# Storing the last 64 rows of a batch pair: one Pool transfer over 128 partitions in place of two Sync transfers over 64

## The chip, the cores and the metric

The kernel runs on one core of one Trainium2 chip. The metric is the device time of one execution in microseconds. Executions of the kernel before take 435.15 to 436.84 us on the days and chips here. The profile's span, from the first to the last instruction, is some 1.7 to 2.2 us shorter than the time. Times of the span below are counted from its start.

## The reference

The program is an attention layer with a forget gate (8 batches, 8 heads, 576 rows, head width 64), followed by a spectral mix over the sequence and a small gate:

```python
    u = x + y                                   # x: attention output, y: irfft of the mixed modes
    return (u + np.maximum(u @ w_ch, 0.0)).astype(np.float32)     # (8, 576, 512)
```

Only this last line and its output matter here. The output is 8 x 576 x 512 float32, 9.4 MB. As 576 = 4 x 128 + 64, each batch has four blocks of 128 rows and one of 64.

## The kernel before: the parts that matter

The last stage works through a list of jobs. A wide job makes one 128-row block of two batches. A job `(b, 4)` makes the last 64 rows of batches b and b+1 in one tile: the lower 64 partitions hold batch b, the upper 64 batch b+1.

```python
        jobs = []
        for b in range(0, B, 2):
            if b == 0:
                jobs += [((c, sb), (c, sb + 1)) for c in (b, b + 1) for sb in (0, 2)]
            else:
                jobs += [((b, sb), (b + 1, sb)) for sb in range(4)]
        jobs += [((b, 4),) for b in range(0, B, 2)]        # last: four jobs of 64 + 64 rows
...
        def emit_o(job, ps, u, o, pair, split=False):
            ...
                nc.vector.scalar_tensor_tensor(o[:, bs, :], ps[1][:, bs, :], 0.0, u[:, bs, :], ALU.max, ALU.add)
                b, sb = job[0]
                if sb == 4:
                    for h in range(2):
                        nc.sync.dma_start(
                            out[b + h, 512:576, :], o[64 * h : 64 * h + 64, 0, :]
                        )
                ...
                elif sb % 2 or n_wide < 2:                 # the wide stores, on Sync too
```

`pool_dma` is a helper that issues a transfer on Pool and keeps it in program order. Pool loads the weights (`wb`) with it and, in the stage before the last one, moves ten small rows (`yl` to `yy`).

The softmax here doesn't subtract the row's maximum and nothing guards it: scores larger than these inputs give would overflow.

## Time and profile before

| | kernel before |
|---|---|
| time, median | 435.68 us (435.57 to 436.04, 5 runs) |
| span of the profiled run | 434.1 us |
| last arithmetic ends | 425.7 us |
| last output data | 432.5 us |
| DMA rate 420 to 424 us / 428 to 432 us | 401 / 221 GB/s |

The prediction shows the lines for these.

### The profile page before, as it was taken

Reading aid. Unit: us, or ns where it says so; the run is one execution under the profiler, and the core shown is the slowest. Engines: PE = TensorE matmul, PEld = TensorE weight load, DVE = VectorE, ACT = ScalarE, POOL = GpSimd, SP = SyncE. Lnnn points to the kernel's source line nnn. Section 1 sums busy time; section 2 is a strip of 40 time slices with the busy share of each in tenths; the row PEclk is TensorE's granted clock in tenths of the full one; section 3 lists DMA queues with packets and bytes.
Section 4 is the critical chain, followed back from the end, with each engine's and each line's share of the span. In section 5 each row is a group of like instructions: output and inputs, shape, how many; then the busy total and the mean of one; then the engine's idle time right before and its main releaser. Section 6 shows DMA issues by size and latency. Waiting matters only on the chain.

```text
span 434.1 us, 12383 instructions
## 1 busy us (share of the span) xinstructions
PE 360.6 (83%) x5338; PEld 249.1 (57%) x5356; DVE 263.5 (61%) x659; ACT 225.5 (52%) x339; POOL 126.9 (29%) x198
## 2 busy tenths in 40 slices
PE   3787799999887977878878797899999977989991
PEld 2353666676665665666656576666665544644540
DVE  5797788876565656555557667533324543743891
ACT  2887478774645446446365454244344432731780
POOL 7333332233233232332323232232232232200400
PEclk9997699997967958668688659699999998989996
DMA  8999999999999999999999999999999999996798
GB/s 181 236 235 237 238 237 238 246 213 217 228 220 237 220 229 232 216 237 227 222 236 212 211 211 211 211 211 213 210 211 211 210 211 211 211 211 130 256 384 257
DMA packets 51086, 97.39 MB, mean 224 GB/s; under 512 B 3799, under 2 KB 12983, under 8 KB 51031
## 3 DMA queue, kind: packets, MB, share of 16 engines
q0 software_dynamic: 46464, 85.65, 101.0%
q1 hardware_dynamic: 4567, 10.95, 7.2%
q8 instruction: 42, 0.69, 0.6%
q14 instruction: 13, 0.11, 0.1%
HBM read 163.73 MB, written 9.44 MB: 399 GB/s over the span
## 4 chain that ended last, share of the span: by engine, by line
DMA 36%; PE 30%; ACT 9%; DVE 8%; issue 4%; POOL 0%; ACTq 0%; DVEq 0%
DMA wb<-in_moe_w_i_dram 36%; ACT E L590 7%; PE pav L628 6%; PE A L191 5%; PE tp L321 5%; PE ps L583 4%; PE vp L555 2%; PE pu L842 2%; DVE QTs L336 2%; ACT KT L334 2%; PE px L671 1%; PE pz L842 1%; DVE os L1019 1%; DVE x_all L650 1%; DVE E L605 1%
## 5 line engine op out<-in xcount | busy, mean ns | idle before, releaser
L590 ACT ACTIVATE E<-ps 128x1024 bf16<-128x1024 f32 (+1 forms) x128 | 100.8, 847 | 27.1 <-PE pav L628 17.1
L191 PE MATMUL A<-XT,wb 128*128 128x16 bf16 x1984 | 71.7, 181 | 11.7 <-DMA wb<-in_moe_w_i_dram 7.1
L191 PEld LDWEIGHTS <-wb 128*128 128x128 bf16 x1984 | 64.2, 99 | 26.0 <-issue 12.2
L96 POOL DMA_DIRECT2D wb<-in_moe_w_r_dram x64 | 42.5, 665 | 120.9 <-PE ps L583 22.0
L96 POOL DMA_DIRECT2D wb<-in_moe_w_i_dram x64 | 42.3, 661 | 85.8 <-DMA wb<-in_moe_w_i_dram 40.1
L583 PE MATMUL ps<-QTs,KT 64*128 64x64 bf16 (+4 forms) x384 | 53.7, 312 | 14.6 <-ACT E L590 12.4
L628 PE MATMUL pav<-va,E 128*128 128x65 bf16 (+1 forms) x1088 | 53.7, 205 | 7.2 <-DVE x_all L650 6.8
L628 PEld LDWEIGHTS <-E 128*128 128x128 bf16 (+1 forms) x1088 | 43.8, 111 | 16.9 <-DVE x_all L650 8.4
L605 DVE TENSOR_TENSOR E<-E,trimask 128x256 bf16<-128x256 bf16 (+2 forms) x128 | 37.0, 304 | 20.0 <-ACT E L590 19.4
L881 ACT CAST XW<-pxw 128x512 bf16<-128x512 f32 x36 | 20.7, 587 | 34.8 <-PE pxw L874 23.4
L340 ACT COPY VT<-tp 128x640 bf16<-128x640 bf16 (+1 forms) x32 | 23.3, 759 | 28.8 <-PE tp L321 28.7
L583 PEld LDWEIGHTS <-KT 64*128 64x128 bf16 x384 | 19.2, 98 | 31.5 <-issue 20.6
L924 ACT CAST XW<-pB 128x512 bf16<-128x512 f32 x36 | 20.9, 586 | 29.8 <-PE pB L842 29.7
L334 ACT COPY KT<-tp 128x640 bf16<-128x640 bf16 (+1 forms) x32 | 22.0, 750 | 26.1 <-PE tp L321 26.0
L923 DVE CAST x_all<-pA 128x512 bf16<-128x512 f32 x36 | 24.9, 692 | 15.4 <-PE pA L842 13.6
L874 PE MATMUL pxw<-wch,yy 128*128 128x512 bf16 x133 | 32.9, 379 | 1.1 <-issue 0.5
L336 DVE COPY QTs<-tp 128x640 bf16<-128x640 bf16 (+1 forms) x32 | 23.3, 767 | 14.1 <-PE tp L321 13.9
L650 DVE TENSOR_TENSOR x_all<-pav,rcp 128x384 bf16<-128x384 f32 x64 | 29.1, 455 | 1.1
L639 DVE RECIPROCAL rcp<-pav 128x6 f32<-128x6 f32 x64 | 12.3, 192 | 25.1 <-PE pav L628 24.3
L842 PEld LDWEIGHTS <-ident_bf 64*64 64x64 bf16 (+1 forms) x336 | 15.6, 109 | 18.4 <-issue 10.7
L555 PE MATMUL vp<-ident_bf,VT 128*128 128x128 bf16 x215 | 21.9, 254 | 5.1 <-DVE QTs L336 4.6
L156 DVE TENSOR_TENSOR YTe<-A,Yacc 128x128 bf16<-128x128 f32 x16 | 5.9, 369 | 32.2 <-PE A L191 32.2
(142 smaller groups left out, 619.1 us busy)
## 6 DMA issues: line engine op xcount, KB each, us to landing
wb<-in_moe_w_r_dram POOLq DMA_DIRECT2D x62, 512.0 KB, 16.9
wb<-in_moe_w_i_dram POOLq DMA_DIRECT2D x62, 512.0 KB, 17.4
stv<-in_v_dram POOLq DMA_DIRECT2D x9, 576.0 KB, 15.6
out_dram<-os SPq DMA_DIRECT2D x10, 512.0 KB, 5.0
stk<-in_k_dram POOLq DMA_DIRECT2D x11, 288.0 KB, 15.6
stq<-in_q_dram POOLq DMA_DIRECT2D x11, 288.0 KB, 15.4
wx<-in_v_dram POOLq DMA_DIRECT2D x5, 576.0 KB, 16.2
out_dram<-uo SPq DMA_DIRECT2D x3, 512.0 KB, 3.2
```

What stands on the lines that cost most here:

```text
L96: keep(nc.gpsimd.dma_start(dst, src))
L191: ins = nc.tensor.matmul(A[:, eb, mi, :], lhsT=w_of(mi, eb * 128), rhs=x_of(m), start=(i == 0), stop=(i == len(terms) - 1),)
L334: nc.scalar.copy(rows(KTs[pr % 2][:, :, 0:S]), tv)
L336: ins = nc.vector.tensor_copy(rows(QT[pr][:, :, :]), tv)
L555: nc.tensor.transpose(vp[:, sc, :, :].rearrange("p b d -> p (b d)"), VTs[s // 2 % 2][:, h, sc * 128 : (sc + 1) * 128], ident_bf[:, :],)
L583: nc.tensor.matmul(ps[:, b, o : o + n], lhsT=KTs[pr % 2][bs, h, jb * 128 : (jb + 1) * 128], rhs=QT[pr][bs, h, jb * 128 + c0 : jb * 128 + c ...
L590: nc.scalar.activation(E[:, :, piece * 512 : piece * 512 + w], ps[:, :, 0:w], ACT.Exp, scale=scale,)
L605: nc.vector.tensor_tensor(dg, dg, tr, ALU.mult)
L628: nc.tensor.matmul(pav[64 * half : 64 * half + w, slot, :], lhsT=E[:, b, c : c + (w - 1) * st + 1 : st], rhs=va[:, jb, b, :], start=(n == ...
L650: nc.vector.tensor_tensor(xo, pi, ri, ALU.mult)
L842: return nc.tensor.matmul(p, lhsT=lhsT, rhs=rhs, start=first, stop=not first, skip_group_check=True)
L874: nc.tensor.matmul(pxw[:, :], lhsT=xT[:, eb, i * 128 : (i + 1) * 128], rhs=wch[:, eb, :], start=(eb == 0), stop=(eb == NDC - 1),)
```

## The change

The intent is to use all 128 partitions in one transfer, to halve the number of issues, and to free Sync.

```diff
                 if sb == 4:
-                    for h in range(2):
-                        nc.sync.dma_start(
-                            out[b + h, 512:576, :], o[64 * h : 64 * h + 64, 0, :]
-                        )
+                    pool_dma(out[b : b + 2, 512:576, :], o[:, 0, :])
```

The source is 128 partitions x 512. The destination is 2 batches x 64 rows x 512: the two batches do not lie next to each other, so the destination can't be walked as 128 equal steps.

## The prediction

> **What bounds the kernel now.** The change touches four groups of stores at the very end, so I read only the tail: first the chain of waits, then the timeline, then the windows and the DMA view.
>
> The chain's last piece (start us, length us, what):
>
> ```profile
> 8 pieces in order of time: start us, us, what
> ...
> 424.99 0.69 DVE uo L1019
> ```
>
> All arithmetic is over at 424.99 + 0.69 = 425.68 us, but the span is 434.1 us. The last 8.4 us hold stores alone; the chain does not follow them. The timeline of the same stretch:
>
> ```profile
> 422.79 1.90 SPq L1039 DMA_DIRECT2D out_dram<-os  x2
> 424.79 6.25 SPq L1026 DMA_DIRECT2D out_dram<-uo  x8
> ```
>
> L1026 is the changed line: eight stores of 64 rows of 2 KB (128 KB). The first could be ready at 422.68 + 0.68 = 423.36, but Sync is still at the wide stores of L1039 until 424.69. Next, the windows (columns: PE, PEld, DVE, ACT, POOL busy; PE clock; DMA share; GB/s):
>
> ```profile
> 411.00:413.00 2.00, 1.74 (x32) 0.89 (x31) 2.00 (x3) 1.66 (x3) 0.00 (x0) 1.00 1.05 381
> 420.00:424.00 4.00, 3.92 (x44) 1.54 (x37) 3.83 (x5) 3.62 (x6) 0.00 (x0) 1.00 1.02 401
> 424.00:427.25 3.25, 0.65 (x5) 0.13 (x3) 1.52 (x3) 0.12 (x1) 0.00 (x0) 0.88 1.02 406
> 428.00:432.00 4.00, 0.00 (x0) 0.00 (x0) 0.00 (x0) 0.00 (x0) 0.00 (x0) 0.50 0.93 221
> 432.50:434.10 1.60, 0.00 (x0) 0.00 (x0) 0.00 (x0) 0.00 (x0) 0.00 (x0) 0.50 0.02 5
> ```
>
> From 420 to 427.25 the DMA engines are full at about 400 GB/s: they work off the wide stores, and the first 64-row stores queue behind these. From about 427.4 to 432.4 the engines are still 93% occupied, but move only 221 GB/s. Then 1.7 us pass in landing and closing. The DMA view of two windows shows that packet size is not the reason. First 411 to 413, where stores of 2 KB rows over 128 partitions run, then 428 to 432, 2 KB rows over 64 partitions:
>
> ```profile
> q1 hardware_dynamic: 390, 0.74, 100.2%
> ```
>
> ```profile
> q1 hardware_dynamic: 526, 0.88, 92.7%
> ```
>
> The first gives 2 us x 16 engines x 1.002 / 390 = 82 ns a packet, the second 4 x 16 x 0.927 / 526 = 113 ns. Same packet, 1.4 times the time (both counts include small semaphore packets). So the bound of the tail is **how fast the 1.05 MB of 64-row stores drain**: 1.05 MB / 0.21 MB per us = 5.0 us, against 2.7 us at the 381 GB/s of the first window. One caution: Sync's own issue is close behind.
>
> ```profile
> L1026 SPq DMA_DIRECT2D out_dram<-uo x8: 525/591/1254, 424.8 to 430.4; - x8
> ...
> DMA to landing us min/median/max: 2.3/2.6/4.1
> ```
>
> 128 KB per 0.59 us is 222 GB/s, so an issue limit and a drain limit are nearly the same number here.
>
> **What the Trainium skill says.** (1) "SBUF — State Buffer", section "Door 1: The DMA port swizzle": partitions 0 to 63 and 64 to 127 each reach only 8 of 16 ports, with an asymptote of about 218 GB/s against 436 for all 128. The trace agrees: 221 against 381 to 406. This is the intent of the change. (2) "DMA: Bandwidth & Descriptors", section "Why a DMA increments its semaphore by 16 and not by 1", on how many engines a transfer uses: the largest number up to 16 that divides the slowest dimension of both access patterns; the software path gives "some direct copies" all 16. The new transfer has a destination of 2 batches x 64 rows and a source of 128 partitions: the rule gives **2 engines**, one per batch, and consecutive engines for the next transfer. No run here shows it yet: every Pool transfer of the kernel before has equal outer counts of 16 or more. (3) The same page, "Issuing engines are not separate DMA queues": Pool's and Sync's transfers share the same 16 engines, so Pool saves issue time alone. (4) "Perfetto Trace Analysis", section "DMA Instruction — SWDGE (GPSIMD)": the end of a Pool transfer in the profile is the end of descriptor writing, not of the data. The trace agrees: 487 ns in the row below, but 1.6 to 3.1 us to landing.
>
> ```profile
> L837 POOL DMA_DIRECT2D yy<-yl x10: 487/487/512, 402.1 to 406.4; - x10
> ```
>
> **The change part by part.** Removed: eight Sync issues, 6.25 us on Sync from 424.79 on. Added: four Pool issues of 256 KB. Pool has been idle since 406.9, so each issue starts right after its DVE result: 423.36, 424.2, 424.9 and 425.68. I take 0.5 to 0.67 us each (the 487 ns above; 661 to 665 ns for the 512 KB weight loads) plus some 0.7 us to the first byte; the fourth moves data from about 427.0. The arithmetic, PE, DVE and ACT are untouched, and no later tile waits for these four buffers. Bytes are the same.
>
> The data, with 2 engines for each transfer (my main case). At 424.0 there are 2.48 MB left, 1.05 of it the 64-row stores, so 1.43 MB of wide stores, 89 KB an engine. At 401 / 16 = 25 GB/s an engine that takes 3.6 us, to 427.5. The four transfers sit on eight engines, 64 rows x 2 KB = 131 KB each, and all have arrived by 427.5, so it does not matter in which order an engine serves its two queues: each of the eight carries 89 + 131 KB. At 82 ns a row the 131 KB take 5.3 us; at the 23 GB/s an engine that 0.74 MB over 2 us gives, 5.7 us; if an engine alone is a little quicker, 5 us. The last data comes at 427.5 + 5.3 = **432.8** (432.4 to 433.2), against 432.4 before. The ports no longer bind, but half of the engines stand idle: the gain is given straight back, to +0.4 us.
>
> The close. Before, the last landing seen by Sync is at 433.0, the end at 434.1. Pool adds something: its drain.
>
> ```profile
> L1155 POOLq DRAIN  x3: 46/102/4721, 406.1 to 433.8; - x3
> ```
>
> The 4721 ns one ends at 410.8, 3.9 us after Pool's last issue (406.88) and 1.3 us after that transfer had landed (409.5). If it counts from the issue, it ends at about 430.3 and is hidden. If it counts from the landing, it ends some 1.3 us after 433.3 or so, and the close slips by about 1 us. I give the second 40%. Sum in the main case: 434.1 + 0.4 (data) + 0.4 (weighted drain) = 434.9 of span, +0.8 us, so 436.5 of time.
>
> **The rivals.** *All 16 engines (22%).* If the Pool transfer is spread over all engines, 1.05 MB drain at about 380 GB/s in 2.7 us: last data 427.5 + 2.7 = 430.2, a gain of 2.2 us, or 1.2 if the drain costs its 1 us: 433.5 to 434.5. For it: the page's exception, and that the change was made on Pool. Against: the page's rule, by which the outer count of 2 decides. *The drain waits for the landing:* above; +1 us on whichever case. *The four transfers fall on the same two engines (3 to 4%):* 4 x 5.3 = 21 us after 427.5, less what overlaps with the wide stores, so an end near 447 to 449 and a loss of 3%. Nothing in the profile speaks for it; the page's cursor speaks against. *Issue was the bound, not the ports:* then freeing Sync helps the transfer, and the number of engines decides all the same, so it moves nothing in the sum.
>
> **Range and chances.** The whole disputed stretch is 5 us of 434, 1.2%; even removing the slow drain completely cannot reach 2%. The mix is 436.5 with about three quarters of the weight and 434 with a fifth, so I say 436.0. The range runs from the full 16-engine gain (433.4) to slower packets plus the whole drain (437.5). Faster by over 2%: 1%. Slower by over 2%: 4%, the same-engines case. Within 2%: 95%.
>
> **What would show it.** In the profile after: (a) L1026 gone from Sync, four Pool transfers of 0.5 to 0.7 us between 423.4 and 426.5; (b) the DMA share in 428 to 432 near 0.5 with about 200 GB/s, if eight engines carry it at full pace; near 1.0 with 380 GB/s and over by 430.3, if all sixteen do; (c) issue to landing of the Pool transfers 6 us or more in the main case, about 4 in the other; (d) Pool's long drain: its end against the last landing tells the two readings apart. I am wrong if the data ends before 431 (engine count), after 435 (engines shared or slower packets), or if anything before 423 us moves.

## More of the kernel before

One more view helps to compare with the kernel after: the DMA strip of the stretch from 423 to 442 us in 40 slices of 0.475 us. The first row is the busy share of the 16 DMA engines in tenths, the second the rate.

```profile
DMA  9999999998999999898500000000000000000000
GB/s 379 397 405 414 414 414 414 414 405 263 259 233 233 224 229 211 194 211 203 121 17 0 0 0 0 0 0 0 0 0 0 0 0 0 0 0 0 0 0 0
```

The reader sees two plateaus: about 410 GB/s until 427.3 us (wide stores), then 194 to 263 GB/s until 432 us (64-row stores), both with the engines nearly always busy.

## The result, and the profile after

The time went from 435.68 us to **443.15 us** (442.82 to 443.66, 5 runs). Ratio 1.0172, interval 1.0157 to 1.0187: slower by 7.5 us, outside the range of 433.4 to 437.5. By the 2% rule it still counts as the same. (A ratio here is the mean time of one kernel's runs over that of the other's of the same rounds, so it is not quite the ratio of the medians quoted.)

The order of work is unchanged: the last arithmetic starts at 425.06 us (before: 424.99). The same DMA strip for the kernel after:

```profile
DMA  9999999498996555937393433354454200000000
GB/s 379 380 397 405 371 431 397 122 193 243 311 277 174 115 90 89 115 97 113 104 130 121 129 112 121 164 181 164 173 132 63 44 9 0 0 0 0 0 0 0
```

The windows of the kernel after (columns as in the prediction; the last two are DMA share and GB/s):

```profile
424.00:428.00 4.00, 0.73 (x6) 0.14 (x3) 1.60 (x3) 0.20 (x1) 2.98 (x4) 1.00 0.94 321
428.00:432.00 4.00, 0.00 (x0) 0.00 (x0) 0.00 (x0) 0.00 (x0) 0.00 (x0) 0.69 0.68 141
432.00:436.00 4.00, 0.00 (x0) 0.00 (x0) 0.00 (x0) 0.00 (x0) 0.00 (x0) 0.50 0.47 132
436.00:440.00 4.00, 0.00 (x0) 0.00 (x0) 0.00 (x0) 0.00 (x0) 0.00 (x0) 0.50 0.24 63
```

The second plateau is gone. As Pool's data starts, the slice from 426.3 us shows only 122 GB/s. The rate comes back to 311 while wide stores are left; from 429 us until 437 it is 89 to 181 GB/s, and in the windows from 432 us on less than half of the engines are busy. The last data comes at 438.4 us. Pool's timeline, and the DMA view of 423 to 442 us for the kernel after:

```profile
423.74 3.26 POOL L96 DMA_DIRECT2D out_dram<-uo  x4 [16.77 <-DVE uo L1019]
```

```profile
DMA packets 2655, 3.01 MB, mean 159 GB/s; under 512 B 1923, under 2 KB 1923, under 8 KB 2655
## 3 DMA queue, kind: packets, MB, share of 16 engines
q1 hardware_dynamic: 543, 1.95, 29.4%
q0 software_dynamic: 2112, 1.06, 24.9%
...
out_dram<-uo POOLq DMA_DIRECT2D x4, 256.0 KB, 13.4
```

Pool's four transfers were issued one after the other from the first DVE result on, as predicted (0.80 to 0.85 us each), but took 13.4 us from issue to landing in the median. And its queue shows 2,112 packets for 512 rows of 2 KB. In the trace's packet records they are 256 packets of 4 KB (two rows each), 64 of 4 bytes (16 for each transfer) and **1,792 of 8 bytes**. No other store in the kernel before or after has such 8-byte packets. 1,792 is 4 x 448, and 448 is 14 x 32: it fits 14 idle engines that each get as many fillers as one of the two working engines has 4 KB packets (64 rows, two to a packet). I call them fillers; what they are for, no view shows, and the records don't name the engine. Each is recorded at 8 ns in the median, 15.7 us in all, which is 1.0 us for each of 16 engines: by their recorded time alone they would not cost much.

Last, the end. The kernel after, its closing line, and Sync's wait:

```profile
L1152 SPq EVENT_SEMAPHORE  x11: 17/28/28, 439.0 to 441.2; - x11
L1152 POOLq DRAIN  x3: 46/102/14419, 426.0 to 441.0; - x3
```

Pool's long drain starts at 426.0 and ends 14.4 us later, at 440.4: 2.0 us after the last data, while Sync's first event after the landing is at 439.0. In the kernel before, whose long Pool drain was over at 410.8, the close took 434.1 - 432.5 = 1.6 us after the last data; now it takes 441.2 - 438.4 = 2.8 us. Of the 7.1 us of span, 5.9 are data and 1.2 are the close.

### The profile page after: what moved, and what is told of

Same layout as the page of the kernel before. It is cut to its first block, busy times and chain, and to the rows that moved or that the text cites. A ratio compares the mean times of both kernels' runs of the same rounds, so it can differ in the third digit from the quotient of the medians.

```text
span 441.2 us, 12397 instructions
## 1 busy us (share of the span) xinstructions
PE 364.8 (83%) x5356; PEld 249.9 (57%) x5356; DVE 264.4 (60%) x659; ACT 225.7 (51%) x339; POOL 129.3 (29%) x202
## 4 chain that ended last, share of the span: by engine, by line
PE 33%; DMA 24%; ACT 10%; DVE 9%; issue 8%; POOL 2%; POOLq 0%; ACTq 0%
DMA wb<-in_moe_w_i_dram 22%; ACT E L590 7%; PE pav L628 6%; PE A L191 6%; PE ps L583 5%; PE tp L321 5%; PE vp L555 3%; PE px L671 2%; DMA stv<-in_v_dram 2%; DVE QTs L336 2%; ACT KT L334 2%; DVE XT L685 2%; DVE E L605 1%; DVE x_all L650 1%; POOL yy L837 1%
## 5 line engine op out<-in xcount | busy, mean ns | idle before, releaser
L590 ACT ACTIVATE E<-ps 128x1024 bf16<-128x1024 f32 (+1 forms) x128 | 100.9, 848 | 28.3 <-PE pav L628 17.4
L583 PE MATMUL ps<-QTs,KT 64*128 64x64 bf16 (+4 forms) x384 | 55.1, 320 | 14.6 <-ACT E L590 12.4
L874 PE MATMUL pxw<-wch,yy 128*128 128x512 bf16 x144 | 35.5, 384 | 0.0
L842 PEld LDWEIGHTS <-ident_bf 64*64 64x64 bf16 (+1 forms) x336 | 15.7, 110 | 18.5 <-issue 10.9
```

What stands on the lines that cost most here:

```text
L583: nc.tensor.matmul(ps[:, b, o : o + n], lhsT=KTs[pr % 2][bs, h, jb * 128 : (jb + 1) * 128], rhs=QT[pr][bs, h, jb * 128 + c0 : jb * 128 + c ...
L590: nc.scalar.activation(E[:, :, piece * 512 : piece * 512 + w], ps[:, :, 0:w], ACT.Exp, scale=scale,)
L874: nc.tensor.matmul(pxw[:, :], lhsT=xT[:, eb, i * 128 : (i + 1) * 128], rhs=wch[:, eb, :], start=(eb == 0), stop=(eb == NDC - 1),)
```

## The experiments

Nine kernels ran. The theory formed from the result: (1) the transfer runs on two engines, because its destination has only 2 outer steps; (2) the fillers that come with this shape on Pool's queue delay the data; (3) Pool's drain waits for the landing. The main rival: Pool's queue is slow for stores, whatever their shape. Each edit below is against the kernel before, or where said against the kernel after.

### e1_pool_halves: the old shape, on Pool

```diff
-                        nc.sync.dma_start(
-                            out[b + h, 512:576, :], o[64 * h : 64 * h + 64, 0, :]
-                        )
+                        pool_dma(out[b + h, 512:576, :], o[64 * h : 64 * h + 64, 0, :])
```

> Edit against the kernel before: the eight 64-row stores keep their form (64 partitions, one batch each) and only move from Sync to Pool. Theory 1 (the loss of 7.5 us comes from the form of the pair transfer: outermost counts 2 against 128, so two DMA engines carry it, and the other engines get 8-byte fillers): this form has 64 against 64, so sixteen engines and no 8-byte packets; the 1.05 MB drain at 210 to 220 GB/s as before, last data at 431.5 to 432.5 us of the span, and Pool's drain, some 1.3 us after the last landing, adds about 1 us: time 436.2 to 437.2. Theory 2 (Pool's queue itself is slow for stores, whatever their form): most of the loss stays, 440 us or more.

Measured: correct, 436.53 us median, ratio 1.0021 (1.0008 to 1.0033). The packet records show no 8-byte packet. Its window and its drain:

```profile
428.00:430.00 2.00, 0.00 (x0) 0.00 (x0) 0.00 (x0) 0.00 (x0) 0.00 (x0) 0.50 1.00 332
```

```profile
L1153 POOLq DRAIN  x3: 46/102/6895, 426.5 to 433.9; - x3
```

So Pool's queue is not slow: with the old shape it costs 0.9 us instead of 7.5. One detail missed: I expected 210 to 220 GB/s, and it was 332. The 64-row stores start beside the wide ones, and the data is in at 431.4, 1.1 us earlier than before (0.45 us of it because this trace's arithmetic ended earlier). The drain (ending at 433.4) gives that back.

This detail says more than it seems to. The last wide packet ended at 429.3 and Pool's last issue at 427.4, so in these two windows 64-row stores run alone:

```profile
429.50:430.00 0.50, 0.00 (x0) 0.00 (x0) 0.00 (x0) 0.00 (x0) 0.00 (x0) 0.50 1.01 361
430.00:430.50 0.50, 0.00 (x0) 0.00 (x0) 0.00 (x0) 0.00 (x0) 0.00 (x0) 0.50 1.04 385
```

With several of them queued, stores of 64 partitions moved 361 to 385 GB/s, a 4 KB packet of two rows taking 159 ns. So 64 partitions in a store do not by themselves hold the tail to 221 GB/s.

### e2_sync_pair: the new shape, on Sync

```diff
-                    for h in range(2):
-                        nc.sync.dma_start(
-                            out[b + h, 512:576, :], o[64 * h : 64 * h + 64, 0, :]
-                        )
+                    nc.sync.dma_start(out[b : b + 2, 512:576, :], o[:, 0, :])
```

> Edit against the kernel before: one transfer of the changed kernel's form (2 batches x 64 rows from 128 partitions), but issued by Sync. Theory 1 with the skill's rule (two engines, on this path always the same lowest two): all four transfers fall on one pair of engines, 4 x 64 rows x 2 KB = 524 KB an engine; at the 25.8 GB/s an engine of a 4 KB packet of 159 ns that is 20.4 us after the wide stores end at 427.5, so last data near 448, time about 451 (449 to 453), and no 8-byte packets. Theory 2 (Pool's queue is slow, the form is innocent): a 128-partition transfer at full rate, about 433.5.

Measured: correct, 452.71 us, ratio 1.0392 (1.0378 to 1.0406). The DMA view from 428 to 449 us:

```profile
DMA packets 509, 1.05 MB, mean 50 GB/s; under 512 B 9, under 2 KB 9, under 8 KB 508
```

50 GB/s is the pace of two engines: from 432 us on the packet records show 24 to 26 rows of 2 KB each us, each taking 84 ns, nearly without a gap, to 449.8 us. So the shape decides, on either queue. On Sync all four transfers share one pair of engines. The Trainium skill ("DMA: Bandwidth & Descriptors", section "Why a DMA increments its semaphore by 16 and not by 1") says that this path takes the lowest-numbered engines, and the pace agrees (the records don't name engines): 4 x 64 rows x 84 ns = 21.5 us one after the other. There are no fillers on this path. The changed kernel, on Pool, spreads its transfers over four pairs: the packet records show eight data packets under way at a time at 435.0 to 436.5 us.

### e3_sync_act: the halves on two queues

```diff
-                        nc.sync.dma_start(
+                        (nc.sync, nc.scalar)[h].dma_start(
```

> Edit against the kernel before: the store of the second batch of each pair is issued by ACT instead of Sync, so two queues issue in parallel. If Sync's issue (0.59 us a store of 128 KB) bounds the tail of the kernel before, the tail's 5.0 us shrink to some 3 us and the time falls to 433.5 to 434. If the 8 ports bound each store and two queues do not mix, it stays at 435.3 to 436. If packets of the two queues alternate on an engine between the lower and the upper partitions, something between, and the 2 KB packets of the tail take less than the 150 ns they take now.

Measured: correct, 435.94 us, ratio 1.0009 (0.9996 to 1.0021): no change of time. But the rate of the tail did change:

```profile
426.00:427.00 1.00, 0.00 (x0) 0.00 (x0) 0.69 (x1) 0.22 (x1) 0.00 (x0) 0.92 0.95 264
428.00:430.00 2.00, 0.00 (x0) 0.00 (x0) 0.00 (x0) 0.00 (x0) 0.00 (x0) 0.50 0.99 321
430.00:432.00 2.00, 0.00 (x0) 0.00 (x0) 0.00 (x0) 0.00 (x0) 0.00 (x0) 0.50 0.86 276
```

Two queues carry the two halves at 276 to 321 GB/s against 221 on one. The rows on Sync's queue took 84 ns each in the median, where the tail's rows of the kernel before took 152. What was gained went into two costs at the start: ACT's issues stood in the way of its last copy, so the last arithmetic began at 426.25 instead of 424.99 (DVE waited 1.2 us for ACT), and the rate fell to 264 GB/s for a microsecond when the second queue joined. This run doesn't settle whether the issue or the ports bound the kernel before: both halves of the pair were now also issued in parallel, but each issue took 1.23 us in the median on either queue, against 0.59 before.

### e4_interleaved: all 128 partitions with a shape that gets 16 engines

Row i of batch b+h is computed into partition 2i+h. The destination can then be walked as 64 rows x 2 batches, with 64 as the outer count. The permutation costs no time that the run shows (the last arithmetic ends at 425.5, before at 425.7): it sits in the weights of the matrix products, whose tiles reuse a constant that is no longer needed.

```diff
+        mix = bas[:, 0:4, :, :].rearrange("p a b c -> p (a b c)").rearrange(
+            "p (j t i k) -> p j t i k", j=2, t=2, k=2)
+        # zeroed, then for t, k in 0, 1 with hs = HS[(t + k) % 2]:
+        #   mix[hs, 0, t, :, k] = ident_bf[hs, hs];  mix[hs, 1, t, :, k] = BIl[hs, 512:576]
...
+            if job[0][1] == 4:         # in terms(): two 128x128 products for four 64x64
+                bp, p = job[0][0] // 2, ps[t][:, 0, :]
+                rows[0].append((p, lhs[0], (x_all, XW)[t][:, bp, 8, :], True))
+                rows[1].append((p, lhs[1], yy[:, 1, bp, t, :], False))
...
-                    for h in range(2):
-                        nc.sync.dma_start(
-                            out[b + h, 512:576, :], o[64 * h : 64 * h + 64, 0, :]
-                        )
+                    nc.sync.dma_start(
+                        out[b : b + 2, 512:576, :].rearrange("h i e -> i h e"), o[:, 0, :])
```

> The intent of the change, with sixteen engines: row i of batch b+h is computed into partition 2i+h (two 128x128 permuted weight tiles instead of four 64x64 ones), and one Sync transfer a pair stores 128 partitions with the destination walked row first, batch second, so the outermost counts are 64 and 128. Theory 1: sixteen engines and all partitions, the four stores drain at 350 to 390 GB/s in 2.7 to 3 us, last data at 430.2 to 430.6, time 433.4 to 434.0, below both kernels. If engines meet on the same partitions' ports in this order of rows: up to 435.7. If the outermost count does not decide: no better than the changed kernel.

Measured: correct, **434.25 us**, ratio 0.9970 (0.9956 to 0.9983). It is 0.3% faster than the kernel before, which the 2% rule calls the same, and 2.0% faster than the kernel after.

```profile
428.00:430.00 2.00, 0.00 (x0) 0.00 (x0) 0.00 (x0) 0.00 (x0) 0.00 (x0) 0.72 0.98 368
430.00:432.00 2.00, 0.00 (x0) 0.00 (x0) 0.00 (x0) 0.00 (x0) 0.00 (x0) 0.50 0.07 27
```

The four stores drain at 368 GB/s, each row taking 85 ns where the kernel before took 152. The gain is 1.3 us by ratio, under the 1.7 to 2.3 expected. The 27 GB/s of the last row is about the pace of one engine: from 430.5 on a single row is under way at a time, to 431.4.

### e5_no_backlog: the kernel after, without wide stores in the queue

```diff
-                elif sb % 2 or n_wide < 2:
+                elif n_wide < 7 and (sb % 2 or n_wide < 2):
```

(Against the kernel after; the result is wrong.)

> Wrong on purpose: the changed kernel without the last six wide stores (3.1 MB), so that Sync's queue is empty when Pool's pair transfers come. Each pair transfer, on its own two engines, needs 32 packets of 159 ns = 5.1 us, some 7 us from issue to landing. Theory A (an engine works through the fillers of the earlier transfers before its own share: up to 96 of them for the fourth): the first lands after 7 us, each later one 1 to 1.6 us later than the one before, the fourth after 10 to 12 us. Theory B (the loss beyond two engines comes from sharing an engine with the backlog of wide stores): all four land after about 7 us, and the last data comes at about 432.5 us of the span. In both Pool's drain ends 1.3 us after the last landing.

Measured: 442.26 us, ratio 1.0141 (1.0120 to 1.0162; two runs). The DMA view of 423 to 441 us:

```profile
q0 software_dynamic: 2112, 1.06, 25.9%
...
out_dram<-uo POOLq DMA_DIRECT2D x4, 256.0 KB, 11.5
```

Taking 3.1 MB of other stores away improved the time by about 1 us only. The backlog is not the main cause. Theory A was nearer, but not in its steps: the first transfer, with nothing before it, landed after 8.2 us (expected 7), and the second after 11.6 already, the last after about 11.7. From the first Pool data packet (424.9) to the last (437.2) 12.4 us pass, where each engine of a pair has 32 x 159 ns = 5.1 us of data. The records show more idle engines than queued work explains: from 426 to 428, when three transfers had been issued and the fourth followed by 426.7, on average fewer than five of the 16 engines have a packet of any kind under way.

### e6_inter_pool: e4's shape, on Pool

The edit is e4's, with `pool_dma` in place of `nc.sync.dma_start`.

> The row-interleaved form of e4_interleaved, its four transfers issued by Pool instead of Sync: outermost counts 64 and 128, so sixteen engines and no 8-byte packets. It differs from e4 (434.25 us) by the queue alone. If Pool costs only its drain (1.3 us after the last landing, against about nothing), it takes 435.0 to 435.6 us. If joining the backlog from a second queue costs as well (in e1 and e3 the engines moved fewer packets for about 1 us when the second queue began), 436 to 436.5. If Pool's earlier issue gains, 434.3.

Measured: correct, 436.25 us, ratio 0.9999 (0.9986 to 1.0012). The DMA view of 423 to 441 us, and the drain:

```profile
q0 software_dynamic: 320, 1.05, 15.8%
...
out_dram<-uo POOLq DMA_DIRECT2D x4, 256.0 KB, 6.2
```

```profile
L1176 POOLq DRAIN  x3: 46/102/7580, 426.0 to 434.1; - x3
```

The same bytes on the same queue with the other shape: 320 packets instead of 2,112, and 6.2 us to landing instead of 13.4. The difference, 1,792, is the number of 8-byte fillers. The data ends at 431.8 (e4: 431.4), the drain at 433.6. Against e4 Pool costs (0.9999 - 0.9970) x 436 = 1.3 us. In the two traces the close after the last data takes 2.6 us on Pool and 1.3 on Sync, and the data ends 0.35 us later, so most of this price is the drain. No dip in the rate was seen when Pool's queue joined.

### e7_last_pair_only: one pair transfer of the kernel after

```diff
-                    pool_dma(out[b : b + 2, 512:576, :], o[:, 0, :])
+                    if b == 6:
+                        pool_dma(out[b : b + 2, 512:576, :], o[:, 0, :])
```

(Against the kernel after. Its output is wrong, which doesn't matter for the time.)

> Wrong on purpose: the changed kernel, but of the four pair transfers only the last pair's is issued, beside the full backlog of wide stores. Theory A (fillers of the earlier transfers delay the later ones): with none before it, this transfer needs 5.1 us after the wide stores' end at 427.5, last data at 432.6 to 433, landing 7 us after its issue, Pool's drain 1.3 us later, span 435.2, time 437. Theory B (the backlog itself slows it): landing still 11 us or more after its issue, time 441 or more.

Measured: 439.09 us, ratio 1.0068 (1.0053 to 1.0083). It is between the theories: 9.5 us to landing. A quarter of the stored bytes already costs 3.0 us against the kernel before.

```profile
q0 software_dynamic: 528, 0.27, 6.1%
...
out_dram<-uo POOLq DMA_DIRECT2D x1, 256.0 KB, 9.5
```

528 packets are 64 of data, 16 semaphore writes and 448 fillers. The packet records show two phases. From 428.2 to 431.4, 15 of the 64 data packets start, some taking up to 1.08 us; the fillers run from 428.2 to 429.8. After that a packet takes 159 ns and the next follows at once, to 435.6 us. The slow phase outlasts both suspects: the last wide packet ends at 429.6 and the last filler at 429.8, yet packets that start at 430.2 and 430.8 still take 0.97 to 0.99 us, with nothing but this transfer's data under way. What slows them, the records don't show.

### e8_last_pair_sync and e9_more_fillers

```diff
# e8, against the kernel after
-                    pool_dma(out[b : b + 2, 512:576, :], o[:, 0, :])
+                    if b == 6:
+                        nc.sync.dma_start(out[b : b + 2, 512:576, :], o[:, 0, :])
# e9, against the kernel after
-                    pool_dma(out[b : b + 2, 512:576, :], o[:, 0, :])
+                    w = D if b == 6 else 4
+                    pool_dma(out[b : b + 2, 512:576, 0:w], o[:, 0, 0:w])
```

> Wrong on purpose: as e7_last_pair_only (only the last pair's transfer is issued, beside the full backlog), but by Sync, so two engines and no 8-byte fillers. Theory A (the fillers stall the data): without them the 64 rows of each engine follow the wide stores without a gap, 64 x 84 ns = 5.4 us after 427.5, last data at 433.0 of the span against 435.6 in e7, time 436 to 436.7. Theory C (two engines at the end of the backlog are slow whatever the queue): last data at 435 or later, time 438 or more.

> Wrong on purpose: as e7_last_pair_only, but the three earlier pairs are issued by Pool as well with 4 of their 512 columns only (16 bytes a row, 2 KB a transfer). The fillers go up about fourfold (448 to some 1,800), the data stays that of e7 within 6 KB. Theory A: the last pair's engines go through the fillers of three transfers first and more stalls fall on their data, so the last data comes 1 to 3 us later than in e7 (436.6 to 438.6 of the span, near the changed kernel's 438.4). If the fillers are harmless, it comes at e7's 435.6.

Measured (both wrong): e8 437.83 us, ratio 1.0043 (1.0024 to 1.0062); e9 441.89 us, ratio 1.0139 (1.0122 to 1.0157). First the rate of e8's DMA view, 423 to 441 us, then e9's view:

```profile
GB/s 391 364 419 382 410 410 419 437 373 355 91 46 36 27 50 50 50 41 46 50 50 55 50 50 36 0 0 0 0 18 0 0 0 0 0 0 0 0 0 0
```

```profile
DMA  9999999979999978525000111101111110000000
GB/s 419 428 401 373 382 410 401 382 237 329 171 257 310 179 71 7 8 4 20 1 0 18 46 55 55 46 36 46 46 55 55 55 55 0 0 0 0 0 0 0
...
out_dram<-uo POOLq DMA_DIRECT2D x1, 256.0 KB, 11.7
out_dram<-uo POOLq DMA_DIRECT2D x3, 2.0 KB, 6.5
```

In e8 the two engines run at their 50 GB/s from 429 on, and the last data comes at 434.2: about 1 us later than expected, and 1.4 us before e7's. In the time e8 lies only 1.1 us below e7, and their intervals overlap (1.0024 to 1.0062 and 1.0053 to 1.0083). In the traces e7's close is 0.7 us longer and its data 1.0 us later, when its later arithmetic (0.4 us) is taken off. So the cost of one transfer's own fillers can't be told apart from the drain by the time. The result lies between theories A and C: the first rows beside the last wide stores took up to 0.56 us each, and only from 429.0 on 84 ns.

e9 is the telling one. Three transfers of 2 KB each, in front of the same last transfer, cost 3.1 us more than e7. For some 3 us, from 429.75 on, the rate is next to nothing. The packet records show two halves. Each tiny transfer has 14 packets of 256 bytes (32 x 8, so I take them for its fillers), 42 in all, and such a packet is under way for **574 ns** in the median, up to 1,127; a 4 KB data packet takes 159. From 430.0 to 430.5 up to 15 of them run at a time, the last until 431.4. The last transfer's data, which starts at 428.2 in e7, starts at 431.2 here; its first packet on each of its two engines takes 1.40 and 1.83 us, and the other engines are nearly empty by then. It ends at 437.9, near the 438.4 of the kernel after. (Its issue came only 0.2 us later than e7's, and the tiny transfers' own data is six packets with 2.2 us in all.) My expectation named the size of the delay (1 to 3 us) rightly, but not the form: the number of 8-byte packets stayed 448, as the other fillers came packed.

The rates without fillers and with them, from the packet records (data of the last stores):

```
kernel   queue  outer counts  data packets    median   longest   8-byte packets
e4       Sync   64 / 128      512 of 2 KB      85 ns     104 ns      0
e6       Pool   64 / 128      256 of 4 KB     173 ns     255 ns      0
e2       Sync    2 / 128      512 of 2 KB      84 ns     625 ns      0
after    Pool    2 / 128      256 of 4 KB     159 ns    2708 ns   1792
```

Data packets of more than 1 us appear only where the short outer count and Pool's queue meet (e5, e7 and e9 have them too), and only there are fillers. That they go together is shown; that the one causes the other is not.

## Why the prediction was wrong

**The read of the kernel before held in part.** The tail is stores alone, and the 64-row stores drain at 221 GB/s. But that their 64 partitions set this rate, as the prediction held, the runs do not bear out: e4 on 128 partitions reached 85 ns a row for 152, and 64-row stores reached 80 (e1, two rows in 159 ns) and 84 to 86 (e3). So e4's gain is not shown to come from the 128 partitions; it also has half as many issues. Sync's issuing, which in the kernel before went on until 431.0, 1.4 us before the last data, is the likelier bound, but no run changed it alone. One reading was also off: the 113 ns a packet average in a fifth of tiny semaphore packets (9 ns); the rows alone took 152 ns in the median, 1.8 times the 85 of the first window and not 1.4.

**Two engines instead of sixteen held.** e2 shows it without any disturbance (50 GB/s), and e4 and e6 show that the outer count of 64 undoes it. The rival "all 16 engines" fell. The prediction's worry that all four transfers might meet on one pair of engines is what Sync does (452.71 us), and not what Pool does.

**The step that failed** is "it does not matter in which order an engine serves its two queues: each of the eight carries 89 + 131 KB", and with it the last data at 432.8. It came at 438.4: the 131 KB, put at 5.3 us, took 11.8 us from Pool's first data packet (426.6) to the last. Sharing the engines with the wide stores is not the reason, as it took 12.4 us without them (e5). The pace of a packet held (159 ns for two rows, 82 ns a row predicted). But 31 of the 256 data packets took over 300 ns, together 17.4 us more than at 159, or 2.2 us for each of eight engines; the remaining 4.5 us or so are late starts and gaps. The sum lacked a term, and one term was mis-sized:

| against the kernel before, by ratio x 436 us | measured | what is added |
|---|---|---|
| e8: one transfer on Sync, two engines, no fillers | +1.9 us | the time two engines need behind the backlog |
| e7: the same, on Pool | +3.0 us | +1.1: Pool's drain and this transfer's slow packets |
| e9: three tiny transfers before it | +6.1 us | +3.1: earlier transfers of this shape, with next to no data |
| after: these three at full size | +7.5 us | +1.4: their data and the form of their fillers |

The missing term is what **a transfer of this shape on Pool's queue costs the other engines**: they come late to their own transfer. e9 shows this with next to no data, and it is the largest item. That the fillers are what delays them is the likely reading (in e9 the last one ends at 431.4 and the last transfer's data begins at 431.2), but no run has fillers without such a transfer, and in the kernel after they are recorded at only 1.0 us an engine. The mis-sized term is the data of two engines: I took the wide stores as ended at 427.5, but in e8 the last wide packet starts at 429.1, and the data ends at 434.2 instead of 432.8.

**The drain counts from the landing.** The prediction gave this 40%, and it is so: in all six kernels that end on Pool it ends 1.7 to 2.0 us after the last data, whether that comes at 431.4 (e1) or 438.4 (after). Price: the close is 0.7 to 1.3 us longer (e7 against e8, e6 against e4).

**The signs named at the end** were useful: (a) held in kind, but an issue took 0.80 to 0.85 us, not 0.5 to 0.7; (b) gave 0.68 and 141 GB/s, neither of the two cases: engines busy without data moving at their pace; (c) 13 us where 6 or more was expected. The last data after 435 was also among them, as "engines shared or slower packets"; each is only a part of what was found.

What stays open: by what means such a transfer delays the others, why its own first packets are slow even alone (e5, e7), and how the 1.1 us between e8 and e7 divide. A rival that no run tests is that Pool hands these transfers to the engines late, so that the engines wait and the fillers only go with it; the idle engines of e5 would fit that too. The intervals of the ratios are 0.6 to 0.8 us to either side, so each step of the table is good to about 1 us. The single traces also differ by up to 1.0 us in when the last arithmetic begins (424.54 in e1, 425.52 in e9; e3 apart).

## What to carry to other kernels

Before merging two transfers into one, look at the outermost count of both sides, not at the number of partitions: a destination of 2 x 64 rows ran at the pace of two engines, whichever queue issued it. If the outer count is small, change the layout so that the long dimension comes first; here the permutation was free inside the weights of a product that ran anyway (434.25 us). And do not move the very last stores to Pool: in these runs its drain made the close 0.7 to 1.3 us longer.

## What the Trainium skill lacked or had wrong

- "DMA: Bandwidth & Descriptors", section "Why a DMA increments its semaphore by 16 and not by 1": the rule for the number of engines held on both queues (two engines: 50 GB/s in e2, two packets at a time in e7). It doesn't say that a Pool transfer on two engines comes with fillers, by their count 32 for each other engine: 448 packets of 8 bytes for a transfer of 64 x 2 rows of 2 KB, or 14 packets of 256 bytes at 574 ns each for one of 16-byte rows.
- "SBUF — State Buffer", section "Can I just issue two DMAs to hit both halves?": it holds that two transfers on the lower and the upper half serialize (+6%). In these stores they do not: in e3, from two queues, the tail moved 276 to 321 GB/s against 221 in the kernel before, and in e1, from Pool's queue alone, 361 to 385.
- No page says that Pool's drain at the end of a program waits for the landing of its stores: in six kernels it ended 1.7 to 2.0 us after the last data, and the close was 0.7 to 1.3 us longer.
